# Six products of zeros on TensorE ahead of the first operands, in a kernel of windowed attention and two feed-forward layers

## The chip, the cores and the metric

The kernel runs on one core of a Trainium2 chip. The metric is device microseconds (us) of one execution, lower is better. A core has five engines with a program each: TensorE (PE, with a weight load PEld before each product), VectorE (DVE), ScalarE (ACT), GpSimd (POOL), and SyncE (SP), which here issues every DMA. Each runs its own instructions in order, and they wait for one another by semaphores.

## The reference, cut to what matters

Sink and window attention over 2 batches, 8 heads, 768 positions and 64 dimensions, then two feed-forward layers over the 1536 rows that it gives, each 512 to 2048 to 512 wide:

```python
scores = q @ k.T / 8
keep = (pos < n_sink) | ((rel >= 0) & (rel < window))   # n_sink 4, window 128
a = softmax(where(keep, scores, -1e9));  x = a @ v
h = x @ w_in;  g = maximum(h, 0) + alpha * minimum(h, 0);  x = g @ w_out     # layer 1
h = x @ w_in;  g = maximum(h, 0) + log1p(exp(-abs(h)));    out = g @ w_out   # layer 2
```

All is float32. The numbers n_sink and window are inputs, known only at run time.

## The kernel before, in words

**The start.** The kernel's function (line 801) writes its first instructions in order by hand. SP issues the DMA of the two numbers into `raw` and four loads of 388 KB each of keys, queries and values (`kqv`): three into `temp`, one into `spare`, which are the operands of the first two attention groups. ACT loads its table. POOL writes constants and index patterns (`masks.count`, line 602) and clears two score buffers. DVE clears a part of each of the eight PSUM banks (line 837), finishes the index patterns (`masks.prepare`, lines 618 and 619), makes the identity matrix (line 614, from an index pattern that POOL writes after line 619), turns `raw` into floats `val` (line 840), compares them with what the fast path can do and reduces that to one number `go` (lines 841 to 843). Then **every engine loads `go` and branches on it** (lines 844 and 846): nothing that stands behind the branch can start on any engine before DVE has written `go`.

```python
for n in range(8):
    V.memset(mem.bank[n][64:128, 256:512], 0.0)
masks.prepare(nc)
masks.identity(nc)
V.tensor_copy(val, raw)
```

**Behind the branch** stands the fast path (line 639), whose operations a planner (`Planned`) orders at build time from estimated costs, dependences and due times; the order on each engine is then fixed. There are 24 attention groups of four 128-query tiles. A group is: scores on PE (line 516, 12 products of 64 by 64 weights into two banks); on DVE a masked copy with a row minimum (line 524); on ACT the exponential with its sum (line 527); on DVE the reciprocals (lines 531, 532); the scaling on DVE (line 541) or ACT (line 539); eight transposes on PE (lines 553, 554); copies out of PSUM (lines 198, 202); the products with the values on PE (line 574); and the split of the result into a rounded part and a rest in float32r (lines 202, 206). The scores, transposes and value products are float32; the feed-forward products (line 317, line 370, line 411) are float32r.

The plan begins with the first twelve groups, while the weights of layer 1 are loaded and converted (lines 282 to 298, on DVE and ACT); then come the feed-forward products, for each chunk of 128 hidden units and each tile of 384 rows 24 of them in layer 1 and 21 in layer 2, with the other twelve groups among those of layer 1.

**What the change touches.** `mem.r[0]` is a float32 tile of 128 by 384 that layer 1 uses for its first activations, much later. `mem.bank[7]` is the last of the eight banks; it is one of those of which DVE clears a part at line 837 (partitions 64 to 127, columns 256 to 511), because the transposes of line 554 write 72 partitions of these columns and the copy out of the bank takes all 128. `TT` is 384.

Of the kernel before, what the change touches and what calls it, by code (L numbers as in the profile page):

```python
# [28 lines left out]
TT = 3 * JB  # L29
# [770 lines left out]
@with_exitstack  # L800
def kernel(
    ctx: ExitStack,
    tc: tile.TileContext,
    kqv: bass.AP,
    nsw: bass.AP,
    w1: bass.AP,
    alpha: bass.AP,
    w2: bass.AP,
    out: bass.AP,
):  # L810
    nc = tc.nc
    V = nc.vector
    mem = Memory(tc, ctx)
    small = ctx.enter_context(tc.tile_pool(name="small", bufs=1))
    raw = small.tile([128, 4], I32, name="raw")
    val = small.tile([128, 4], F32, name="val")
    lim = small.tile([1, 2, 4], F32, name="lim")
    okt = small.tile([1, 8], F32, name="okt")
    go = small.tile([1, 1], I32, name="go")
    neg = small.tile([128, 2, 2], F32, name="neg")  # L820

    with tc.manual_schedule():
        nc.sync.dma_start(out=raw, in_=nsw.partition_broadcast(128))
        first = Window(mem, InOrder(nc), kqv)
        first.load(0, 0)
        first.load(1, 0)
        nc.scalar.preload_act_table_set("natural_log_exp_and_others")
        nc.gpsimd.memset(lim, 0.0)
        nc.gpsimd.memset(lim[:, 0, 2:3], 1.0)
        nc.gpsimd.memset(lim[:, 1, 0:1], float(NSK))  # L830
        nc.gpsimd.memset(lim[:, 1, 2:3], 128.0)
        masks = Masks(mem)
        masks.count(nc)
        for s, _ in mem.s[0:2]:
            nc.gpsimd.memset(s[:, :, 0:64], 0.0)
# [5 lines that stand above are left out]
        V.tensor_tensor(okt[:, 0:4], val[0:1], lim[:, 0], ALU.is_ge)  # L841
        V.tensor_tensor(okt[:, 4:8], val[0:1], lim[:, 1], ALU.is_le)
        V.tensor_reduce(go, okt, AX.X, ALU.min)
        fast = nc.values_load(go[0:1, 0:1], min_val=0, max_val=1,
                              skip_runtime_bounds_check_because="a minimum of comparisons is 0 or 1")
    with tc.If(fast > 0) as cmp:
        with tc.manual_schedule(), ExitStack() as own:
            mem.open(tc, own)
            fast_path(tc, mem, masks, val, kqv, alpha, (w1, w2), out, 2)
    with cmp.Else():  # L850
        two = val.rearrange("p (n w) -> p n w", w=2)
        V.tensor_scalar(neg[:, :, 0], two[:, :, 0], 0.0, 4294967296.0, ALU.is_lt, ALU.mult)
        V.tensor_tensor(neg[:, :, 1], neg[:, :, 0], two[:, :, 0], ALU.add)
        V.scalar_tensor_tensor(mem.lims, two[:, :, 1], 4294967296.0, neg[:, :, 1], ALU.mult, ALU.add)
        with ExitStack() as own:
            mem.open(tc, own)
            general_path(tc, mem, kqv, alpha, (w1, w2), out)
# [52 lines left out]
```

## Time and profile before

| | |
|---|---|
| median of 3 runs | 636.86 us (636.72, 636.86, 638.86) |
| the profiled execution | 637.52 us, of which the span from the first instruction to the last is 635.7 us |
| PE busy | 615.2 us (97% of the span), 4192 products |
| DVE, ACT, POOL busy | 478.5 us (75%), 328.9 us (52%), 2.5 us |
| PE's share of the chain that ended last | 90% |
| mean granted TensorE clock | 0.997 of full speed |

"Busy" is the time in which an engine's instructions execute; products are pipelined, so the duration of one is longer than the distance to the next. In the timeline a row is: start, duration, engine, line, operation, output and input, count, and in brackets how long the engine had sat idle before it and what ended that. A row with a count merges instructions that follow one another. In the table of stretches, each engine's busy time stands with its number of instructions, then PEclk, the granted TensorE clock as a share of full speed, then the share and the rate of the DMA engines. The chain of waits is read backwards from the last instruction, and is printed in order of time.

### The profile page before, as it was taken

To read this page: it belongs to the slowest core of one execution; us is meant where nothing else is said; L and a number is where in the kernel's file an instruction comes from. 1 tells how busy PE (TensorE), PEld (TensorE's weight loads), DVE (VectorE), ACT (ScalarE), POOL (GpSimd) and SP (SyncE) were. 2 spreads that over 40 slices of the span, in tenths; PEclk is the share of its full clock that TensorE was granted. 3 is DMA by queue.
4 is the path that set the end of the run, shared out by engine and by line. 5 is a ranking of instruction groups with operands and counts; after the bars stand their busy time and mean duration, and the time that the engine had idled before them with its cause. 6 is when DMAs were issued, how large, how long until landed. Compare 5 with 4: busy or idle time off the path is not lost.

```text
span 635.7 us, 10814 instructions
## 1 busy us (share of the span) xinstructions
PE 615.2 (97%) x4192; PEld 572.1 (90%) x4192; DVE 478.5 (75%) x1119; ACT 328.9 (52%) x739; POOL 2.5 (0%) x18
## 2 busy tenths in 40 slices
PE   5789999999999999999999989999999999999996
PEld 4678999999999999999999979999999999999995
DVE  7999999955345644499966999867876777677774
ACT  4999687644533654356534765433443433343332
POOL 1000000000000000000000000000000000000000
PEclk9999999999999999999999999999999999999998
DMA  8999701121211110176007610000010100000001
GB/s 319 357 385 410 268 1 52 51 77 51 85 51 68 52 51 2 67 249 215 1 1 265 219 46 1 1 1 1 0 51 0 51 1 1 1 25 26 2 0 56
DMA packets 15035, 56.55 MB, mean 89 GB/s; under 512 B 1920, under 2 KB 4480, under 8 KB 14976
## 3 DMA queue, kind: packets, MB, share of 16 engines
q1 hardware_dynamic: 14976, 55.78, 24.5%
q8 instruction: 35, 0.57, 0.4%
q14 instruction: 24, 0.20, 0.1%
HBM read 52.63 MB, written 3.15 MB: 88 GB/s over the span
## 4 chain that ended last, share of the span: by engine, by line
PE 90%; DVE 4%; ACT 3%; issue 1%; DMA 1%; SPq 0%; ACTq 0%; DVEq 0%
PE bank L317 40%; PE bank L411 21%; PE bank L370 19%; PE bank L574 3%; PE bank L516 3%; PE bank L553 2%; PE bank L554 2%; DVE temp L298 1%; DMA temp<-kqv 1%; ACT early L527 1%; DVE g L206 0%; DVE w L206 0%; DVE r L335 0%; ACT temp L282 0%; ACT late L527 0%
## 5 line engine op out<-in xcount | busy, mean ns | idle before, releaser
L317 PE MATMUL bank<-x,w 128*128 128x384 f32 x1536 | 294.5, 337 | 2.8 <-DVE late L357 2.8
L317 PEld LDWEIGHTS bank<-x,w 128*128 128x128 f32 x1536 | 269.2, 188 | 9.7 <-DVE late L357 3.2
L370 PE MATMUL bank<-g,w 128*128 128x384 f32 x768 | 149.3, 338 | 0.0
L411 PE MATMUL bank<-w,g 128*128 128x512 f32 x576 | 143.1, 393 | 0.0
L370 PEld LDWEIGHTS bank<-g,w 128*128 128x128 f32 x768 | 133.3, 188 | 1.4
L411 PEld LDWEIGHTS bank<-w,g 128*128 128x128 f32 x576 | 107.1, 188 | 19.6
L352 ACT ACTIVATE late<-bank 128x384 f32<-128x384 f32 x64 | 31.4, 491 | 113.3 <-PE bank L317 113.3
L335 DVE SCALAR_TENSOR_TENSOR r<-r,alpha,r 128x384 f32<-128x384 f32 x64 | 39.3, 614 | 45.1 <-ACT r L334 44.8
L333 ACT ACTIVATE r<-bank 128x384 f32<-128x384 f32 x64 | 31.3, 490 | 61.7 <-PE bank L317 59.9
L350 DVE TENSOR_SCALAR late<-late 128x384 f32<-128x384 f32 x64 | 22.9, 358 | 44.0 <-ACT late L353 44.0
L355 ACT ACTIVATE late<-late 128x384 f32<-128x384 f32 x64 | 33.7, 526 | 26.1 <-DVE late L350 26.0
L527 ACT ACTIVATE late<-late,st 128x200 f32<-128x200 f32 (+1 forms) x72 | 31.8, 445 | 25.0 <-DVE st L524 25.0
L206 DVE TENSOR_TENSOR g<-late,g 128x384 fp32r<-128x384 f32 x64 | 35.6, 557 | 6.1 <-DVE g L202 0.9
L298 DVE SCALAR_TENSOR_TENSOR temp<-w,temp 128x1024 int32<-128x1024 int32 x32 | 38.8, 1215 | 1.5 <-ACT temp L282 1.5
L206 DVE TENSOR_TENSOR w<-temp,w 128x1024 fp32r<-128x1024 f32 x32 | 39.0, 1218 | 0.1
L198 ACT ACTIVATE w<-temp 128x1024 fp32r<-128x1024 f32 x32 | 34.0, 1064 | 8.1 <-DVE temp L298 8.1
L356 DVE SCALAR_TENSOR_TENSOR late<-late 128x384 f32<-128x384 f32 x64 | 35.6, 557 | 1.9
L206 DVE TENSOR_TENSOR late<-late 128x384 f32<-128x384 f32 x64 | 35.5, 557 | 1.8
L206 DVE TENSOR_TENSOR g<-r,g 128x384 fp32r<-128x384 f32 x64 | 35.5, 555 | 1.6 <-ACT g L198 0.4
L357 DVE SCALAR_TENSOR_TENSOR late<-bank,late 128x384 f32<-128x384 f32 x64 | 35.5, 556 | 0.1
L198 ACT ACTIVATE late<-bank 128x512 f32<-128x512 f32 (+2 forms) x49 | 24.8, 543 | 19.7 <-PE bank L554 14.4
L353 ACT ACTIVATE late<-late 128x384 f32<-128x384 f32 x64 | 33.6, 525 | 1.9
(98 smaller groups left out, 524.6 us busy)
## 6 DMA issues: line engine op xcount, KB each, us to landing
w<-w SPq DMA_DIRECT2D x32, 1023.8 KB, 5.8
w<-kqv SPq DMA_DIRECT2D x20, 388.0 KB, 7.3
late<-kqv SPq DMA_DIRECT2D x20, 388.0 KB, 3.5
out<-late SPq DMA_DIRECT2D x18, 128.0 KB, 1.7
spare<-kqv SPq DMA_DIRECT2D x5, 388.0 KB, 4.5
temp<-kqv SPq DMA_DIRECT2D x3, 388.0 KB, 4.4
out<-early SPq DMA_DIRECT2D x2, 256.0 KB, 3.0
out<-early SPq DMA_DIRECT2D x2, 128.0 KB, 3.9
```

Source lines behind the costliest of these rows:

```text
L198: nc.scalar.activation(out, src, AF.Copy)
L206: engine(nc, e).tensor_tensor(out, a, b, ALU.subtract)
L298: add(lambda nc, e: nc.vector.scalar_tensor_tensor(b, raw[0].rearrange("p n w -> p (n w)").bitcast(I32)[:, 0:2048:2], 13, b, ALU.logical_s ...
L317: nc.tensor.matmul(out=h, lhsT=w[:, a, kk], rhs=xt[:, b, kk], start=(kk == 0 and n == 0), stop=(kk == 3 and n == 2))
L335: add(lambda nc, e: nc.vector.scalar_tensor_tensor(n, n, mem.alpha[:, c:c + 1], r, ALU.mult, ALU.add), {"DVE": 0.54}, [("r", 0), ("alpha", ...
L353: add(lambda nc, e: nc.scalar.activation(u, u, AF.Exp, scale=-1.0), {"ACT": 0.43}, [], [ku], due)
L355: add(lambda nc, e: nc.scalar.activation(l, w, AF.Ln), {"ACT": 0.43}, [kw], [kl], due)
L356: add(lambda nc, e: nc.vector.scalar_tensor_tensor(u, w, 1.0, u, ALU.subtract, ALU.subtract), {"DVE": 0.47}, [kw], [ku], due)
L357: add(lambda nc, e: nc.vector.scalar_tensor_tensor(l, h, 0.0, l, ALU.max, ALU.add), {"DVE": 0.47}, [kh], [kl], due)
L370: nc.tensor.matmul(out=self.mem.bank[m][:, 0:TT], lhsT=w[:, a, m], rhs=g[:, b], start=(ends[0] and part == 0 and n == 0), stop=(ends[1] an ...
L411: nc.tensor.matmul(out=self.mem.bank[bk], lhsT=g[:, a, m * 128:(m + 1) * 128], rhs=w[:, b], start=(c == 0 and part == 0 and n == 0), stop= ...
L527: add(lambda nc, e, u=u: nc.scalar.activation(s[:, u, c0:], s[:, u, c0:], AF.Exp, bias=st[:, 0, u:u + 1], scale=-1.0, accum_out=st[:, 1, u ...
```

## The change

Between the construction of the masks and the index patterns, three statements are added: DVE clears `mem.r[0]`, and PE multiplies the first 128 columns of that tile with the whole of it, six times, each time into columns 0 to 383 of bank 7. Nothing reads the result.

```diff
         masks = Masks(mem)
+        V.memset(mem.r[0], 0.0)
+        for n in range(6):
+            nc.tensor.matmul(out=mem.bank[7][:, 0:TT], lhsT=mem.r[0][:, 0:128], rhs=mem.r[0], start=True, stop=True)
         masks.count(nc)
```

On PE the six products come ahead of the load of `go`. Before (`bank_61` and `bank_62` are banks 0 and 1; in brackets the semaphores an instruction waits for):

```order
L906 UNCONDITIONAL_BRANCH [waits barrier_Pool_Activation_PE_DVE_SP_release]
L844 TENSOR_LOAD go [waits DVE_49]
L846 COMPARE_AND_BRANCH
L516 MATMUL bank_61<-temp 64x136 [waits DMAHW1_49,DVE_49]
L516 MATMUL bank_62<-temp 64x136 [waits DVE_49]
L516 MATMUL bank_61<-temp 64x128
```

And now, where `r_69` is `mem.r[0]` and `bank_68` is bank 7:

```order
L909 UNCONDITIONAL_BRANCH [waits barrier_Pool_Activation_PE_DVE_SP_release]
L835 MATMUL bank_68<-r_69 128x384 [waits DVE_49]
L835 MATMUL bank_68<-r_69 128x384 x5
L847 TENSOR_LOAD go [waits DVE_49]
L849 COMPARE_AND_BRANCH
L516 MATMUL bank_61<-temp 64x136 [waits DMAHW1_49,DVE_49]
```

The first product waits for DVE, which has to clear the tile; behind the sixth stand the load of `go` and the first scores, as before.

On DVE, the end of the eight clearings (`bank_67` and `bank_68` are banks 6 and 7) and all that stands ahead of the branch, before:

```order
L837 MEMSET bank_67 64x256
L837 MEMSET bank_68 64x256
L618 TENSOR_SCALAR late<-late 128x192 [waits Pool_49]
L619 TENSOR_TENSOR late<-late 128x192 [waits DVE_49]
L614 TENSOR_SCALAR ident<-late 128x128 [waits Pool_49]
L840 CAST val<-raw 128x4 [waits DMAHW0_49]
L841 TENSOR_TENSOR okt<-val,lim 1x4 [waits DVE_49]
L842 TENSOR_TENSOR okt<-val,lim 1x4
L843 TENSOR_REDUCE go<-okt 1x1 [waits DVE_49]
L844 TENSOR_LOAD go [waits DVE_49]
```

And now:

```order
L840 MEMSET bank_67 64x256
L840 MEMSET bank_68 64x256 [waits PE_49]
L618 TENSOR_SCALAR late<-late 128x192 [waits Pool_49]
L619 TENSOR_TENSOR late<-late 128x192 [waits DVE_49]
L614 TENSOR_SCALAR ident<-late 128x128 [waits Pool_49]
L843 CAST val<-raw 128x4 [waits DMAHW0_49]
L844 TENSOR_TENSOR okt<-val,lim 1x4 [waits DVE_49]
L845 TENSOR_TENSOR okt<-val,lim 1x4
L846 TENSOR_REDUCE go<-okt 1x1 [waits DVE_49]
L847 TENSOR_LOAD go [waits DVE_49]
```

The order of these is the same, but the clearing of bank 7 now waits for PE. The new clearing of `r` stands ahead of the eight, as DVE's first instruction behind the barrier.

## Rows read from the trace of the kernel before

**Rows 1.** The table of stretches, from the start to the PE-bound part:

```profile
0.00:5.50 5.50, 0.00 (x0) 0.00 (x0) 3.42 (x16) 1.28 (x1) 2.16 (x17) 1.00 0.54 155
...
10.40:14.50 4.10, 4.02 (x35) 3.59 (x36) 3.20 (x18) 2.47 (x10) 0.00 (x0) 1.00 1.03 412
...
16.00:38.00 22.00, 16.87 (x278) 13.02 (x278) 21.95 (x88) 21.58 (x67) 0.00 (x0) 1.00 0.98 373
38.00:300.00 262.00, 262.00 (x2126) 249.76 (x2123) 188.62 (x466) 155.10 (x374) 0.31 (x1) 1.00 0.34 120
```

**Rows 2.** The chain of waits at the start (start, us, what):

```profile
1.18 3.90 DMA temp<-kqv
...
5.58 1.61 PE bank L516 x20
```

**Rows 3.** Timeline of the start, DVE, SP and PE:

```profile
0.86 2.19 DVE L837 MEMSET bank<- 64x256 f32 x8 [0.86 <-PEq L903]
...
2.59 0.43 SPq L477 DMA_DIRECT2D spare<-kqv  x1
...
4.54 0.15 DVE L843 TENSOR_REDUCE go<-okt 1x1 int32<-1x8 f32 x1
5.41 4.13 SPq L477 DMA_DIRECT2D w<-kqv  x8
5.45 0.21 DVE L625 TENSOR_SCALAR late<-late,val 128x1 f32<-128x1 f32 x1 [0.76 <-DVE go L843]
...
5.58 2.56 PE L516 MATMUL bank<-temp 64*64 64x136 f32 x36 [5.58 <-DMA temp<-kqv]
...
7.22 0.30 DVE L524 CUSTOM_DVE_ANT_0 late<-bank,mask 128x136 f32<-128x136 f32 x1 [0.62 <-PE bank L516]
```

**Rows 4.** Timeline of PE around 14.5 us:

```profile
10.48 1.83 PE L516 MATMUL bank<-w 64*64 64x200 f32 x24 [1.48 <-DVE st L531]
...
12.51 0.23 PEld L553 LDWEIGHTS bank<-ident,late 128*128 128x128 f32 x1
12.72 0.42 PE L553 MATMUL bank<-ident,late 128*128 128x128 f32 x1
12.94 0.42 PE L554 MATMUL bank<-ident,late 128*72 128x128 f32 x1
...
14.80 0.92 PE L516 MATMUL bank<-w 64*64 64x200 f32 x24
...
15.92 0.27 PE L553 MATMUL bank<-ident,early 128*128 128x128 f32 x1
16.03 0.27 PE L554 MATMUL bank<-ident,early 128*72 128x128 f32 x1
```

**Rows 5.** PE by line and form, window 5 to 14.4 us:

```profile
L516 PE MATMUL bank<-temp 64*64 64x136 f32 x12 | 2.0, 452 | 5.6 <-DMA temp<-kqv 5.6
...
L516 PE MATMUL bank<-temp 64*64 64x72 f32 x12 | 1.4, 324 | 0.0
```

**Rows 6.** Stretches of PE's longest later gap and after its last product:

```profile
367.70:370.50 2.80, 0.03 (x1) 0.00 (x1) 2.80 (x6) 1.69 (x3) 0.00 (x0) 1.00 0.00 0
630.00:631.00 1.00, 0.14 (x1) 0.00 (x0) 0.00 (x0) 0.66 (x2) 0.00 (x0) 1.00 0.88 324
...
632.00:632.50 0.50, 0.00 (x0) 0.00 (x0) 0.00 (x0) 0.00 (x0) 0.00 (x0) 0.86 0.80 260
632.50:633.00 0.50, 0.00 (x0) 0.00 (x0) 0.00 (x0) 0.00 (x0) 0.00 (x0) 0.50 0.12 43
```

**Rows 7.** The load into `spare` until 15 us, from issue to landing:

```profile
DMA to landing us min/median/max: 5.4/5.4/5.4
```

**Rows 8.** The loads into `w` until 15 us, from issue to landing:

```profile
DMA to landing us min/median/max: 4.9/7.8/10.8
```

**Rows 9.** Timeline of DVE where it waits for PE:

```profile
9.03 0.30 DVE L524 CUSTOM_DVE_ANT_0 early<-bank,mask 128x136 f32<-128x136 f32 x1 [0.85 <-PE bank L516]
...
14.24 0.69 DVE L202 COPY late<-bank 128x512 f32<-128x512 f32 x1 [0.68 <-PE bank L554]
```

## The prediction

> **What bounds the kernel now.** I read the table of stretches first. PE does nothing until 5.5 us; from 16 to 38 us DVE is busy for 21.95 of 22.00 us and ACT for 21.58, while PE has gaps; from 38 us on PE is busy without a gap that the view shows [rows 1]. Neither of these stretches has slack that could swallow a later start: all that they work on is released behind the branch on `go`. So the kernel is a start, then a filled pipeline, and what moves the branch moves the end, unless the first dozen microseconds behind it get shorter.
>
> Then the chain of waits and the timeline of the start. The chain names the load of `temp` (issued at 1.18, landed 3.90 later, at 5.08 us) as what the first scores at 5.58 us waited for [rows 2], but the branch comes just as late: DVE clears the banks in eight times 0.27 us from 0.86 to 3.05, writes `go` at 4.54 to 4.69, and the first instructions behind the branch start 0.76 us later, on SP at 5.41, on DVE at 5.45, on PE at 5.58 [rows 3]. The last clearing, that of bank 7, begins at 0.86 + 2.19 - 0.27 = 2.78 us; from there to PE's first scores it is 2.8 us, all of it one chain on DVE with one step on POOL.
>
> Last, PE itself. A group's 24 score records take 1.83 us at 10.48, and the same work takes 0.92 us at 14.80; transposes follow one another by 0.22 us near 12.8 us and by 0.11 us near 16 [rows 4]. [...] PE therefore runs at half rate from 5.58 us until about 14.5 us. It rose after PE had worked without a pause from 10.48 on, some 4.0 us; the 3.4 us of work from 5.58 to about 9.0 (10.48 less the 1.48 us that it sat idle) had not raised it.
>
> **The change part by part.** *The clearing of `mem.r[0]`* puts 384 elements ahead of DVE's eight. At the clearings' 272 ns for 256 that is 0.41 us, done at 0.86 + 0.41 = 1.27. As the clearing of bank 7 has to wait anyway, this delays nothing else; with 0.1 us for the semaphore PE starts at about 1.4 us.
>
> *The six products.* No row shows a float32 product of 128 by 128 weights. [...] That is both ends: PE finishes between 1.4 + 3.8 = 5.2 and 1.4 + 7.7 = 9.1 us. [...] What I take follows the one rise in the trace: half rate for 4.0 us, to 5.4 us, then the remaining 3.7 us of work at full rate, 1.8 us: PE finishes at 7.2 us. If the rise comes earlier or later by a microsecond, the finish moves by half of one.
>
> The weight loads of these products lie beside them, as the 0.23 us load at 12.51 lies beside the transposes' even steps [rows 4], so I cost them at nothing; without that cover twelve of them would add 2.8 us, which the bound above does not hold and I think unlikely.
>
> [...]
>
> *The wait that comes with them.* The last of the eight clearings writes columns 256 to 511 of bank 7, and the products write 0 to 383, so DVE now waits there for the sixth product. What is queued behind that clearing on DVE is everything up to `go`, and for `go` wait all five engines, SP with its next loads among them. The four loads that SP has issued ahead of the branch go on; no other does. With PE done at 7.2 us the clearing starts at 7.3 and PE's first scores 2.8 us later, at 10.1 instead of 5.58: **4.5 us later**. By the two ends it is 8.1 to 12.0, that is 2.5 to 6.4 us later.
>
> *What the later branch gives back.* The first four loads have then long landed. Before, `spare` landed at 2.59 + 5.4 = 8.0 us [rows 3, 7], in the middle of the second group's scores, which ran at half rate just as slowly, so this alone gives perhaps 0.1 us. The first load behind the branch took 4.9 us or more [rows 8], queued behind those four; on an empty queue I give it the 3.9 us of `temp` [rows 2], about 1 us less, which shortens the third group's start but not the scaling and the transposes beside it: some 0.3 us.
>
> *What the clock gives back.* If PE is at the upper level behind the branch, its work is shorter by half, but only what DVE and ACT wait for counts, since they are the bound right after. DVE waits for PE in three places before 16 us: 0.62 us at 7.22 [rows 3], 0.85 at 9.03 and 0.68 at 14.24 [rows 9], together **2.15 us**. That is the most, and nothing is the least. In its way stands the pause that the change itself makes: PE idles 2.9 us between the sixth product and the first scores, and after that waits for loads and for DVE again. The trace shows both answers: the clock stayed up over an idle stretch of 2.77 us at 367.7 us, and at the end it had begun to fall within 632.0 to 632.5, where the mean is 0.86 and then 0.50, some 2.2 us after PE's last product at 630.14 [rows 6]. So the level behind the branch is open, and if it holds there, the sparse work that follows may lose it before the transposes. I take a part, 0.2 us, besides the 0.4 us of the loads, 0.6 in all, near the least because the pause is longer than both that the trace shows.
>
> [...]
>
> Sum: the profiled execution's 637.52 us (span 635.7 and 1.8 around it) + 4.5 - 0.6 = 641.4; it lies 0.66 us above the median of the runs, so against the median 636.86 + 3.9 = **640.8 us**. A measurement of this kernel can tell about 0.5% from no change, 3.2 us here: above 640.0 or below 633.7.
>
> **The rivals.**
> *The clock holds through the first groups.* The products raise it, the pause does not lower it, and the scores and transposes of the first groups run at the upper level. For it: the 2.77 us of idling that changed nothing. Against it: the fall at the end after 2.2 us. Then 2.15 us and 0.4 come off: 636.86 + 4.5 - 2.5 = 638.9, within 0.5%.
> *The clock does not rise within the six products*, as it didn't in the 3.4 us of the first scores. PE finishes at 9.1, the branch is 6.4 us late, and the loads give 0.4 back: 642.9 us. For it: the trace's only rise took about nine microseconds from PE's first product. Against it: that work had the pause of 1.48 us, and the six have none.
> *Not slower: the products are short.* If each is one record at half rate, or the array takes zeros in 128 by 128 form at full rate from the start, PE is done at 5.2 us, and the branch is 2.5 us late; with the clock held and the loads earlier this comes back: 636.86 + 2.5 - 2.5 = 636.9. It decides from a finish of PE before 2.7 + 2.5 = 5.2 us. For it: no row shows such a product; against it, the two records of each score product. A cover further down that swallows the late start would end at the same time; with DVE at 21.95 of 22.00 us from 16 us on and PE without gaps behind it I see none.
> **How the numbers follow.** Forecast 0.55, its own range 639.3 to 642.3 (PE done between 6.5 and 8.5 us, so 3.8 to 5.8 later, with 1.4 back at the low end and 0.4 at the high one); clock held 0.23; no rise 0.14; short products and a cover 0.08. The range that holds eight in ten runs from 638.7, just under the held clock, to 643.0, the case without a rise. Slower by over 0.5% is above 640.0: about four fifths of the forecast (0.45), all of the third (0.14) and a little of the held clock (0.05), 0.64. Faster by over 0.5% would need 3.2 us of gain, more than the 2.5 us that can come back: 0.03. The rest, 0.33, is within.
>
> **What would show it.** Six products on PE from about 1.4 us, in 12 records, by 0.64 us at first and 0.32 after a rise. DVE idle before the clearing of bank 7, released by PE, for about 3.9 us (from 3.4 to 7.3). `go` at about 9.1 us, PE's first scores and SP's next loads near 10. Behind that, the distance of the transposes, 0.21 or 0.11 us, tells which level they ran at, and DVE's three waits for PE tell what came back. From about 20 us on the two traces should run side by side with one constant shift, about 3.9 us. I am wrong if `go` comes before 7 us, if the clearing of bank 7 does not wait, or if the shift at 20 us is not the shift of the end.

## The result, and the profile after

The changed kernel took 643.94 us (median of 7 runs, 641.94 to 644.80), the kernel before in the same series 638.66 us (7 runs, 636.72 to 641.66): the ratio is **1.0072, 95% interval 1.005 to 1.0094**, some 4.6 us slower (3.2 to 6.0; the two medians lie 5.28 us apart, which this interval holds). The forecast of 640.8 us had the direction; the time lies above its range, which ended at 643.0.

The profiled execution took 643.94 us as well, with a span of 642.0. Its timeline of the start, for DVE, PE and SP, answers to [rows 3] (same columns):

```profile
0.88 0.38 DVE L833 MEMSET r<- 128x384 f32 x1 [0.88 <-PEq L906]
...
1.31 1.92 DVE L840 MEMSET bank<- 64x256 f32 x7
...
1.32 6.71 PE L835 MATMUL bank<-r 128*128 128x384 f32 x12 [1.32 <-DVE r L833]
...
8.16 0.27 DVE L840 MEMSET bank<- 64x256 f32 x1 [4.93 <-PE bank L835]
...
9.92 0.15 DVE L846 TENSOR_REDUCE go<-okt 1x1 int32<-1x8 f32 x1
10.79 3.70 SPq L477 DMA_DIRECT2D w<-kqv  x8
10.82 0.21 DVE L625 TENSOR_SCALAR late<-late,val 128x1 f32<-128x1 f32 x1 [0.76 <-DVE go L846]
...
10.96 1.03 PE L516 MATMUL bank<-temp 64*64 64x136 f32 x30 [2.93 <-DVE go L846]
```

The six products are 12 records. Their weight loads, in the timeline of PEld, show the steps:

```profile
5.32 0.33 PEld L835 LDWEIGHTS bank<-r 128*128 128x128 f32 x1 [0.31 <-issue]
5.96 0.33 PEld L835 LDWEIGHTS bank<-r 128*128 128x128 f32 x1 [0.31 <-issue]
6.58 0.84 PEld L835 LDWEIGHTS bank<-r 128*128 128x128 f32 x3 [0.28 <-issue]
```

Up to here they went by 0.64 us, and the last ones came faster, by 0.32 us (at 6.58, 6.90 and 7.22): PE worked at half rate for more than 5 us, and finished at 8.03. DVE sits idle for 4.93 us ahead of the clearing of bank 7, and then everything stands as before, **5.38 us later**: `go` at 9.92 against 4.54, the loads at 10.79 against 5.41, the scores at 10.96 against 5.58.

The timeline of PE further on answers to [rows 4]:

```profile
14.17 0.57 PE L516 MATMUL bank<-w 64*64 64x200 f32 x12 [1.60 <-DMA w<-kqv]
15.06 0.57 PE L516 MATMUL bank<-w 64*64 64x200 f32 x12 [0.33 <-DMA w<-kqv]
...
15.84 0.27 PE L553 MATMUL bank<-ident,late 128*128 128x128 f32 x1
15.95 0.27 PE L554 MATMUL bank<-ident,late 128*72 128x128 f32 x1
```

The first transposes already follow one another by 0.11 us, the upper level. The clock that the products raised had held over 2.93 us of idling. DVE's three waits for PE are gone: its copy that began at 14.24 us [rows 9] now begins at 17.50, only 3.26 us later, so 2.12 of the 5.38 us have come back. How much of that is the clock's, this profile alone can't tell (e3 below can). Then comes a wait that the kernel before did not have. From the timeline of DVE, the first conversion of weights, before and after:

```profile
20.67 0.32 DVE L541 TENSOR_SCALAR late<-late,st 128x200 f32<-128x200 f32 x1
20.90 0.69 DVE L291 TENSOR_SCALAR temp<-w 128x1024 bf16<-128x1024 bf16 x1
```

```profile
17.50 0.68 DVE L202 COPY late<-bank 128x512 f32<-128x512 f32 x1
...
23.68 0.32 DVE L541 TENSOR_SCALAR late<-late,st 128x200 f32<-128x200 f32 x1
25.63 0.69 DVE L291 TENSOR_SCALAR temp<-w 128x1024 bf16<-128x1024 bf16 x1 [1.63 <-DMA w<-w]
```

The weights are not there: 1.63 us of idling for `w<-w`, and the distance to the kernel before goes from 3.01 us (23.68 against 20.67) to 4.73. The load landed at 25.5 us, against 19.7 before: it was issued 4.18 us later (14.54 against 10.36) and took 11.0 us instead of 9.3. The table of stretches of the profile after shows why (DMA share and GB/s are the last two columns):

```profile
3.00:7.00 4.00, 4.00 (x8) 2.04 (x8) 0.23 (x1) 0.00 (x0) 0.00 (x0) 1.00 0.94 357
7.00:8.00 1.00, 1.00 (x4) 0.28 (x2) 0.00 (x0) 0.00 (x0) 0.00 (x0) 1.00 0.23 90
8.00:11.00 3.00, 0.07 (x5) 0.07 (x5) 1.64 (x9) 0.00 (x0) 0.24 (x1) 1.00 0.00 0
...
12.50:16.00 3.50, 1.57 (x30) 1.31 (x29) 3.36 (x25) 3.24 (x16) 0.00 (x0) 1.00 0.95 347
```

The DMA engines, at a share of 1.03 behind the branch of the kernel before [rows 1], run dry for some four microseconds: the first four loads are through, and the next ones wait for `go`.

The profiles differ by 6.3 us in span, 1.6 more than at line 291. The rest is elsewhere: where layer 2 begins, PE waits some 2.8 us for DVE in both. Before and after, from PE's timeline:

```profile
370.50 2.87 PE L317 MATMUL bank<-x,w 128*128 128x384 f32 x15 [2.77 <-DVE late L357]
```

```profile
375.31 4.37 PE L317 MATMUL bank<-x,w 128*128 128x384 f32 x15 [2.79 <-DVE late L357]
```

The same 15 products take 2.87 and 4.37 us. The stretches of the profile after have the granted clock (third number from the right) there at half:

```profile
375.00:376.00 1.00, 0.69 (x2) 0.69 (x3) 1.00 (x3) 0.00 (x0) 0.00 (x0) 0.59 0.00 0
376.00:378.00 2.00, 2.00 (x8) 2.00 (x7) 2.00 (x4) 0.99 (x2) 0.00 (x0) 0.50 0.00 0
378.00:379.00 1.00, 1.00 (x5) 1.00 (x5) 1.00 (x3) 0.00 (x0) 0.00 (x0) 0.70 0.00 0
```

In the profile before it is 1.00 from 370 to 380 us. From the start of these products to the end it is 265.2 us before and 266.7 after. The experiments had to tell whether that belongs to the change.

### The profile page after: what moved, and what is told of

Read it like the earlier page. It is cut to its first block, busy times and chain, and to the rows that moved or that the text cites. A ratio compares the mean times of both kernels' runs of the same rounds, so it can differ in the third digit from the quotient of the medians.

```text
span 642.0 us, 10839 instructions
## 1 busy us (share of the span) xinstructions
PE 620.6 (97%) x4204; PEld 574.4 (89%) x4204; DVE 478.5 (75%) x1120; ACT 329.0 (51%) x739; POOL 2.5 (0%) x18
## 4 chain that ended last, share of the span: by engine, by line
PE 92%; DVE 3%; ACT 3%; issue 1%; DVEq 0%; POOL 0%; ACTq 0%
PE bank L317 42%; PE bank L370 21%; PE bank L411 20%; PE bank L574 3%; PE bank L516 2%; PE bank L553 1%; PE bank L554 1%; PE bank L835 1%; ACT late L527 1%; ACT early L527 1%; ACT late L198 0%; ACT temp L282 0%; ACT w L198 0%; DVE early L387 0%; ACT early L539 0%
## 5 line engine op out<-in xcount | busy, mean ns | idle before, releaser
L411 PEld LDWEIGHTS bank<-w,g 128*128 128x128 f32 x576 | 107.1, 188 | 19.7 <-DVE g L206 0.2
```

The lines of the kernel that those rows point to most:

```text
L411: nc.tensor.matmul(out=self.mem.bank[bk], lhsT=g[:, a, m * 128:(m + 1) * 128], rhs=w[:, b], start=(c == 0 and part == 0 and n == 0), stop= ...
```

## The experiments

Theory A: what costs is that `go`, and with it SP's next loads, comes late. Theory B: what costs is the late start of PE and DVE. Theory C: the clock that the products raise gives back 2 us or more. All were timed beside the kernel before (12 runs, or 6 for the two with the largest effects). The table has for each the ratio with its interval, and from its profile the start of line 291's first conversion, the start of layer 2's products behind the gap, and the time from there to the end of the span.

| kernel | median us (before's) | ratio, 95% interval | line 291 | gap ends | from there to the end |
|---|---|---|---|---|---|
| before | | | 20.90 | 370.50 | 265.2 |
| the change | 643.94 (638.66) | 1.0072, 1.005 to 1.0094 | 25.63 | 375.31 | 266.7 |
| e1_clear_first | 638.67 (638.78) | 1.0009, 0.9991 to 1.0027 | 21.38 | 371.00 | 265.1 |
| e2_eight_short | 638.63 (638.78) | 1.0001, 0.9982 to 1.002 | 20.34 | 369.60 | 265.2 |
| e3_delay_only | 643.25 (638.78) | 1.0072, 1.0044 to 1.0099 | 26.30 | 376.64 | 266.7 |
| e4_twelve | 646.97 (638.78) | 1.013, 1.0098 to 1.0162 | 28.86 | 379.18 | 266.7 |
| e5_sp_late | 641.57 (638.82) | 1.0046, 1.003 to 1.0061 | 24.56 | 373.84 | 267.2 |
| e6_go_first | 640.44 (638.82) | 1.0023, 1.0003 to 1.0043 | 22.42 | 371.83 | 266.8 |
| e7_fill_gap | 637.32 (638.82) | 0.9972, 0.9957 to 0.9988 | 22.2 | 371.82 | 265.1 |
| e8_short_and_fill | 637.20 (638.68) | 0.9982, 0.9966 to 0.9997 | 20.7 | 369.95 | 265.1 |
| e9_change_and_fill | 642.23 (638.68) | 1.0045, 1.003 to 1.006 | 25.3 | 375.57 | 265.4 |

From line 291 to the end of the gap every profile has 349.2 to 350.3 us. So the start decides when line 291 begins, and the rest follows at a fixed distance, but for the last column, which has two values.

**e1_clear_first**: the products without the wait on DVE.

```diff
         masks = Masks(mem)
+        V.memset(mem.bank[7][64:128, 256:512], 0.0)
         V.memset(mem.r[0], 0.0)
...
-        for n in range(8):
+        for n in range(7):
             V.memset(mem.bank[n][64:128, 256:512], 0.0)
```

> The clearing of bank 7 is put ahead of the six products, so DVE no longer waits for PE; the products themselves stay, and PE alone reaches the branch late, at about 8.4 us. Theory A (the cost is that `go`, and with it SP's next loads, comes 5.4 us late): `go` at about 5 us, loads issued at 5.6 to 5.8 us, first scores near 9.1 us at the upper clock level, and the time 0 to 1.5 us above the kernel before, against 4.7 for the change; the first conversion of weights (line 291) starts no later than 1.5 us after its 20.9 us of before. Theory B (the cost is PE's own time for the products): the scores come 3.5 us late and the end moves by 3 to 3.5 us.

The six products are all there, and nothing measurable is lost: 1.0009. `go` came at 5.05 us. Here is its PE, from the timeline:

```profile
1.64 5.71 PE L836 MATMUL bank<-r 128*128 128x384 f32 x12 [1.64 <-DVE r L834]
7.28 1.03 PE L516 MATMUL bank<-temp 64*64 64x136 f32 x30
...
9.77 0.57 PE L516 MATMUL bank<-w 64*64 64x200 f32 x12 [0.89 <-DVE st L524]
11.79 0.94 PE L516 MATMUL bank<-w 64*64 64x200 f32 x12 [1.45 <-DMA w<-kqv]
...
12.94 0.42 PE L554 MATMUL bank<-ident,late 128*72 128x128 f32 x1
13.15 0.42 PE L553 MATMUL bank<-ident,late 128*128 128x128 f32 x1
```

The products took 5.71 us, a microsecond less than in the change, so the scores came at 7.28, earlier than expected. They ran at the upper level; then PE waited for loads twice (the first release is named DVE, but the load landed at 9.6 us, just ahead of the scores at 9.77), and the second part of the third group and the transposes ran at half rate again (0.94 for 0.57, 0.21 us from one transpose to the next). Theory B asked for 3 us and is out for PE's own time.

**e2_eight_short**: what the clock alone is worth. Beside the clearing of bank 7 as in e1:

```diff
-        V.memset(mem.r[0], 0.0)
-        for n in range(6):
-            nc.tensor.matmul(out=mem.bank[7][:, 0:TT], lhsT=mem.r[0][:, 0:128], rhs=mem.r[0], start=True, stop=True)
+        V.memset(mem.r[0][:, 0:128], 0.0)
+        for n in range(8):
+            nc.tensor.matmul(out=mem.bank[7][:, 0:128], lhsT=mem.r[0][:, 0:128], rhs=mem.r[0][:, 0:128], start=True, stop=True)
```

> Bank 7 is cleared first, and instead of six products of 384 columns there are eight of 128 columns, some 3.4 us at half rate, which are over at about 4.8 us, when `go` is written: nobody waits for them. It asks what the clock alone is worth. Theory A: if the upper level comes before the transposes of the first groups, DVE's three waits shrink by up to 2.1 us, but the first weights land at about 19.7 us, 1.2 us before the conversion that needs them (20.9 us), so no more than 1.2 us is gained: time 1.2 to 0 us below the kernel before. If the level does not rise earlier: no change within 0.5 us. Theory C (the clock is worth the full 2.1 us or more): 2 us or more below.

No change that can be measured. The first scores still ran at half rate; the rise came among the transposes, near 13.3 us against 14.5, and line 291 began at 20.34, 0.56 us earlier. Theory C did not show.

**e3_delay_only**: the late branch without products.

```diff
         masks = Masks(mem)
+        for t in (mem.r[0], mem.early[:, 1600:3072], mem.r[1], mem.late[:, 3136:4608], mem.early[:, 800:1600], mem.r[0], mem.r[1][:, 0:128]):
+            V.memset(t, 0.0)
         masks.count(nc)
```

> No products; instead DVE does 5.4 us of clearings of unused space ahead of the eight banks, so `go` comes as late as in the change, and PE comes to the first scores cold. Theory A (late branch, DMA stream decides): 4.7 to 5.6 us above the kernel before, as much as the change or up to 0.9 us more; the conversion at line 291 waits for its DMA as in the change, or for 0.5 us less. Theory C (the warm clock gives back 2 us or more in the change): 6.5 us or more above before.

The same ratio as the change, 1.0072. `go` came at 9.87, PE began its scores at 10.91 and at half rate, and DVE again ended up waiting for the weights:

```profile
26.30 0.69 DVE L291 TENSOR_SCALAR temp<-w 128x1024 bf16<-128x1024 bf16 x1 [1.68 <-DMA w<-w]
```

That is 0.67 us later than in the change, so the products' clock was worth at most that in these two profiles, and nothing that the times can tell. **The delay alone accounts for the whole cost, as far as six runs can tell.**

Its timeline of PE and DVE also shows where most of the 2.12 us of the change come from:

```profile
10.91 1.82 PE L516 MATMUL bank<-temp 64*64 64x136 f32 x30 [10.91 <-DVE go L845]
...
13.96 1.81 PE L516 MATMUL bank<-w 64*64 64x200 f32 x24
...
16.21 0.27 PE L554 MATMUL bank<-ident,late 128*72 128x128 f32 x1
16.32 0.27 PE L553 MATMUL bank<-ident,late 128*128 128x128 f32 x1
...
18.12 0.68 DVE L202 COPY late<-bank 128x512 f32<-128x512 f32 x1
```

`go` was 5.33 us late, and the copy of [rows 9] begins 3.88 us late: 1.45 us came back without any product. With the branch late, the loads are there when PE wants them; the third group's lands at 13.84 us, 3.1 after its issue. PE goes through the scores of three groups, from 10.91 to 15.8 us, without the 1.48 us of idling of [rows 4], and by this work of its own it is at the upper level when the transposes come (0.11 us apart). DVE's three waits are 0.62 us, 0.37 and nothing, against 0.62, 0.85 and 0.68. That leaves some 0.67 of the 2.12 us for the clock that the products raised.

**e4_twelve**: the change with `range(12)`.

> Twelve products instead of six. Theory A: the six more run at the upper level, 0.32 us a record pair half, 0.64 us each, 3.8 us in all, and each moves `go` by its whole length: 8.5 us above the kernel before (4.7 + 3.8). Rival (the warmer clock or the wait that follows swallows a part): less than 7 us above.

The products took 9.68 us instead of 6.71, 2.97 more, and not the 3.8 expected, because the clock rose earlier in this profile, by the steps of 0.64 and 0.32 us after an estimated six records instead of nine; `go` came 2.97 us later than in the change (12.89 against 9.92), line 291 3.23 us later, and the time is 8.3 us above the kernel before (1.013). The upper level was lost again near 15 us, within the scores of the second group, and the transposes ran at half rate (0.21 us apart). Each further microsecond of products still costs about one: 3.7 us of time for 2.97, by the two ratios.

**e5_sp_late**: only SP is late.

```diff
         masks.identity(nc)
+        for t in (mem.early[:, 1600:3072], mem.late[:, 3136:4608], mem.r[0], mem.r[1], mem.early[:, 800:1600], mem.alpha):
+            nc.gpsimd.memset(t, 0.0)
+        nc.sync.dma_start(out=mem.alpha, in_=alpha)
         V.tensor_copy(val, raw)
```

> The kernel before, without products and without any wait on DVE or PE; SP alone is held back: behind its first four loads it waits for a row of clearings on GpSimd that begin once the identity is made, and so issues its next loads near 10.8 us, as in the change. Theory A (what the change costs is the late loads): the conversion at line 291 waits for the first weights and starts 4.5 to 5 us after its 20.9 us, and the time is 4.2 to 5 us above the kernel before, as for the change. Theory B (PE's and DVE's late start is the cost): within 1.5 us of the kernel before.

GpSimd was quicker than I had reckoned, so the loads came 3.83 us late, not 5.4. From the timeline, SP and PE:

```profile
9.24 4.16 SPq L477 DMA_DIRECT2D w<-kqv  x8
...
12.61 0.94 PE L516 MATMUL bank<-w 64*64 64x200 f32 x12 [3.05 <-DVE st L532]
```

And from the view of the loads into `w`, in a window that holds the first of these eight alone:

```profile
DMA to landing us min/median/max: 3.2/3.2/3.2
```

The wait arose one step ahead of where I expected it: at the scores of the third group, which need the first load behind the branch. (The release named is DVE, but that load landed at 9.24 + 3.2 = 12.44 us and the scores follow 0.17 us behind it; before, it took 4.9 us and landed at 10.31, again 0.17 us ahead of the scores.) Line 291 followed 3.66 us late without a wait of its own, and the time is 2.9 us above the kernel before.

SP was not quite alone in being late, though. While GpSimd cleared, DVE's instructions beside it took longer, and `go` came 1.04 us late:

```profile
3.86 1.33 POOL L841 MEMSET early<- 128x1472 f32 x1
...
3.95 1.31 DVE L614 TENSOR_SCALAR ident<-late 128x128 f32<-128x128 f32 x1 [0.34 <-POOL late L613]
4.09 1.18 DVE L843 CAST val<-raw 128x4 f32<-128x4 int32 x1
...
5.58 0.15 DVE L846 TENSOR_REDUCE go<-okt 1x1 int32<-1x8 f32 x1
```

In the kernel before, the same two DVE instructions take 0.23 and 0.16 us. By what e6 shows next for PE and DVE, an estimated 0.5 of the 2.9 us belongs to this; the late loads cost the other 2.4, some two thirds of their lateness.

**e6_go_first**: the counterpart, `go` on time, PE and DVE late.

```diff
-        for n in range(8):
+        for n in range(7):
             V.memset(mem.bank[n][64:128, 256:512], 0.0)
...
         V.tensor_reduce(go, okt, AX.X, ALU.min)
+        V.memset(mem.bank[7][64:128, 256:512], 0.0)
```

> The change with one line moved: the clearing of bank 7, which waits for the six products, stands behind the computation of `go` on DVE, so SP, ACT and GpSimd branch on time while PE and DVE branch as late as the sixth product allows. It is the counterpart of the kernel in which only SP is late. Theory A: DVE starts on its masks 3 to 4 us late and wins 2 us of that back from the upper clock level, so line 291 starts 0.5 to 2 us after 20.9 and the time is 0.5 to 2 us above the kernel before. Theory B: 4 us or more above.

From its timeline, SP, DVE and PE:

```profile
5.58 4.04 SPq L477 DMA_DIRECT2D w<-kqv  x8
...
8.19 0.27 DVE L847 MEMSET bank<- 64x256 f32 x1 [3.32 <-PE bank L835]
8.83 0.21 DVE L625 TENSOR_SCALAR late<-late,val 128x1 f32<-128x1 f32 x1 [0.37 <-issue]
...
13.60 0.42 PE L553 MATMUL bank<-ident,late 128*128 128x128 f32 x1
13.81 0.42 PE L554 MATMUL bank<-ident,late 128*72 128x128 f32 x1
```

SP issued its loads at 5.58 us; DVE waited 3.32 us for the products and started on its masks at 8.83 us against 5.45, 3.4 us late; line 291 began 1.5 us late, and the time is 1.5 us above (1.0023, 1.0003 to 1.0043). Of 3.4 us late, 1.9 are made up, because the loads were there. The clock is only a part of that: the first scores ran at the upper level, but the transposes at half rate again (0.21 us apart), and the run does not separate it from what e3 regains without products. So theory B holds a little too, at less than half a microsecond for each. It is the time that carries this, within 0.2 to 2.7 us, and not line 291 of one profile: in e7, whose start is that of the kernel before, line 291 began at 22.2 us.

**e7_fill_gap**: the kernel before, with products in the gap at layer 2's start. (They are planned behind the first chunk's `g2_out`; three of the ten came to stand between its products. Bank 7 is not in use then.)

```diff
+    def fill(self, p, due, count):
+        g, kg, bank = self.mem.g[p % 3], ("g", p % 3), self.mem.bank[7]
+        for n in range(count):
+            self.p.add(lambda nc, e: nc.tensor.matmul(out=bank, lhsT=g[:, 0, 0:128], rhs=self.weight(1, 0)[:, 0], start=True, stop=True),
+                       {"PE": 0.22}, [kg + (0,), kg + (1,), ("w", 0, 0)], [("bank", 7)], due)
...
         ffn.g2_out(t, c, p, d + 1)
+        if p == 0:
+            ffn.fill(p, d + 3.0, 10)
```

> The kernel before, its start untouched. Ten products of 512 columns into bank 7, then unused, are put where layer 2 begins, three ahead of the last products of its first chunk and seven into PE's gap of 2.4 to 2.8 us near 370 us. It tests whether the spread of the runs (636.3 to 641.7 us) comes from the clock, which in the profile of the change fell in that gap for 3.2 us and in the profile of the kernel before did not. If so: the slow end of the runs goes, the median falls by 1 to 2 us and the profile shows full rate after the gap. If not: the spread stays and the median moves by no more than 0.7 us.

Faster than the kernel before: 0.9972, 0.9957 to 0.9988, the median by 1.5 us. PE's timeline of the gap:

```profile
369.58 1.75 PE L420 MATMUL bank<-w,g 128*128 128x512 f32 x7
371.82 2.90 PE L317 MATMUL bank<-x,w 128*128 128x384 f32 x15 [0.49 <-DVE late L357]
```

PE idles 0.49 us instead of 2.4 to 2.8, and the 15 products run at full rate. The spread did not vanish (636.21 to 639.19, before 636.57 to 641.26); a part of it lies at the start, where line 291 began at 22.2 us in this profile against 20.90 though nothing there was changed. That the gain is a fall of the clock that no longer happens is argued, from the price of a fall in other profiles (1.5 to 2.0 us, the last column of the table): the one profile of the kernel before has no fall in the gap.

**e8_short_and_fill** and **e9_change_and_fill**: e2 and the change, each with nine such products, all behind the first chunk's last one (the operations of `fill` read banks 0 to 2 in the plan as well).

> The kernel with eight short products that nobody waits for, and nine products of 512 columns in PE's gap where layer 2 begins, all of them after the first chunk's last product. If the fall of the clock in that gap is what spreads the runs, the median is 1.5 to 2.5 us below the kernel before (0.2 to 0.4%), as with the gap filled alone or a little more, since none of the nine delays a product that is waited for; the short products add 0 to 0.6 us of gain. If the short products cost something after all, less than 1.5 us.

> The change, with the same nine products in the gap near 375 us. The two effects should add: 4.7 us for the late branch, less 1.5 to 2 us for the gap, so 2.7 to 3.2 us above the kernel before (ratio 1.0042 to 1.005), and in its profile the conversion at line 291 near 25.6 us and the span 614 to 615 us longer than that start. If the fall of the clock had a part in the 4.6 us that the change costs, the sum comes out lower, under 2.5 us.

The second came out as expected: 2.9 us above the kernel before by its ratio, 1.0045. The late branch and the filled gap add up, as far as these intervals tell: filled against filled, the change is 4.9 us slower (642.23 against e7's 637.32, from different series). The first gave 1.5 us by the medians and 1.1 by the ratio, at the foot of what I expected and no better than the gap filled alone: the short products add nothing that can be measured. Its profile shows why; DVE's first conversion already waits for its load:

```profile
DVE temp L291 <- DMA w<-w: 0.4, 1, 0.4
```

That is at 20.7 us, where the kernel before began without waiting, at 20.90. In this profile a quicker start of PE runs into the loads at once.

## Why the prediction was wrong

*The wait on bank 7, and what is queued behind it*: right. All of it moved, by one amount, and e3 shows that this alone costs 1.0072; e1 shows that the products without it cost nothing that can be measured.

*The six products*: the price of 0.64 us a record at half rate was right, and so were two records a product. The 7.7 us of work at half rate and the 3.8 at full rate from which PE's finish is summed were my estimate; no run shows the twelve records at one rate throughout, and in their place the profile after shows steps of 0.64 us at first (7.7 for twelve), 0.32 at the end, and 6.71 us in all. The 0.1 us for the semaphore was 0.06 (`r` cleared at 1.26 us, PE at 1.32). The step that was mis-sized is "half rate for 4.0 us". The records went by 0.64 us until about 6.6 us, more than 5 us after the first, and PE finished at 8.03 instead of 7.2: the branch was 5.38 us late and not 4.5, which was inside the bounds of 2.5 to 6.4. The twelve records took 6.71 us here, 5.71 in e1, 5.98 in e9 and 6.74 in e6; the one rise of the trace before was no measure.

*What comes back*: the 0.6 us forecast and the 0.65 measured at line 291 (5.38 less 4.73) agree by accident. This is the step whose mechanism failed. The sum had 0.4 us for loads that are there sooner, 0.2 for the clock, and nothing for a later wait on the weights. Measured, 2.12 us had come back by the copy at 17.5 us. Of these, 1.45 come back without any product (e3), because the loads have landed and PE works on without a pause; the first load behind the branch took 3.2 us instead of 4.9, and I had put 3.9. The clock that the products raised adds some 0.67 and not the 2.15 of its three waits. Then the weights took 1.6 us back. I had priced a single load and not the stream: the four microseconds in which the DMA engines have nothing to do come out at the first weights. A quicker start would have met the same limit, since those weights landed only 1.2 us ahead of line 291 in the profile before (19.7 against 20.90) and behind it in e8's. And so "one constant shift" from about 20 us on was wrong: 3.01 just ahead of line 291 (23.68 against 20.67), 4.73 at it, 4.81 at 375 us.

*The rival "the clock holds"* had the clock right in this profile, but counted all three waits as the clock's and would have needed its 2.5 us to last; in e4 (by 15.12 us, the second group's scores) and e6 (by 13.60, the transposes), behind such products, the level was lost within the first groups; *"no rise"* had a time nearer to the one measured (642.9) but not the mechanism; *"short products"* is out.

*The base of the sum* is the step that put the time out of the range. The three runs shown had a median of 636.86; seven have 638.66, and 29 in one later series 638.82. The forecast of 3.9 us above the kernel before lies within the measured 3.2 to 6.0; 640.8 was 1.8 us low before the change was counted. On the base of 638.66 the sum is 642.6, and the range, moved by as much, would have held the measured time. Of the 3.1 us that were missing, 1.8 are this, 0.8 the size of the delay, and the remaining 0.5 is within what the runs leave open. A range around a sum has to hold the spread of the runs that it starts from, and mine held only that of the costs.

*The fall in the gap* (1.5 us in this pair of profiles) is nothing that the times put down to the change: filling the gap gains as much with it (1.0072 to 1.0045) as without (1 to 0.9972). The profiles alone would say otherwise. Of those whose gap is not filled, all five that start late have the fall (the change, e3 to e6), and the three others have not (before, e1, e2); why is open.

## What to carry to other kernels

Work on an idle engine is free only if nothing waits for it: before adding it, look at which buffer it writes and who writes that next, here a clearing that stood ahead of a branch on which all five engines wait. When something delays the issue of loads, price the stream and not the single transfer: ask whether the DMA queues run dry, and which consumer has the least slack behind them. A wait that a faster engine gives back counts only up to the next operand that isn't there yet. And before a gain is put down to the faster engine, run the delay without it: here two thirds of what came back in the first groups came back all the same (e3).

## What the runs showed of the hardware

The clock's rise came after different amounts of the same work: the 12 records of zeros took 5.71 us in one profile (e1) and 6.74 in another (e6), so a microsecond of PE's finish can't be foreseen. Zeros raised the clock as the scores and transposes of the kernel before did: the records went from 0.64 to 0.32 us apart in the change, the transposes there from 0.21 to 0.11.

The fall is as variable. Behind nearly the same pause of PE, the upper level held in the change (2.93 us of idling, then 1.60 and 0.33, until 15.06 us, with transposes by 0.11 us behind it) and was lost in e4 within the scores that follow (2.96 us of idling before 13.95; near 15 us eight records of 128 columns take 0.89 us instead of 0.51). The idle stretch at the start of layer 2 was 2.77 us (before), 2.74 (e1) and 2.38 (e2) without a fall, and 2.79 (the change), 2.38 (e3, e4, e6) and 2.44 (e5) with one, at a price of 1.5 to 2.0 us each time. In these profiles such a gap can cost the full rate: 2.4 us was enough in four of them, and 2.8 us was harmless in one. Filling the gap with products that nothing reads (e7, and e8 with it) was the only edit that made this kernel faster.

The view's clock column shows 1.00 over the first 10 us of the kernel before, the change and e2, where PE's first records run at half rate (0.64 us apart in the change); what the records take tells the level there. In the fall at layer 2's start it agrees with them: 0.50 from 376 to 378 us in the change, where the 15 products take 4.37 us instead of 2.87.

In e5, DVE's instructions of 0.23 and 0.16 us took 1.31 and 1.18 while a clearing of 1.33 us ran on GpSimd.
